# Masked key tiles and gate columns by small SBUF-to-SBUF transfers on the SP queue, with corrected planner durations

## The chip, the cores and the metric

The kernel runs on one core of one Trainium2 chip (trn2). The metric is the device time of one execution in microseconds. All runs quoted are of the fast state, as far as the state of a one-core run can be told: no run was over 1.5% above the fastest of its kernel.

Engines are called as in the profile. PE is TensorE, PEld its weight loads, DVE is VectorE, ACT is ScalarE, POOL is GpSimd. SP is SyncE; here it does nothing but issue transfers, in order, and wait for semaphores.

## The reference, cut to what matters

The input is x of 2048 tokens by 512. Two branches are mixed by a gate per token, `g = sigmoid(sum(x * gate_w))`:

```python
# branch A: attention with 32 heads of 16, in 4 chunks (L = 512), with a running memory
logits = einsum('bhqd,bhkd->bhqk', qs, ks) * scale + mask     # causal inside the chunk
a_dot  = einsum('bhqk,bhkd->bhqd', softmax(logits), vs)
num    = einsum('bhld,bhde->bhle', phi(qs), M)                # memory read; phi = elu + 1
den    = einsum('bhld,bhd->bhl', phi(qs), z)
o      = sig(beta) * num / (den + 1e-6) + (1 - sig(beta)) * a_dot
M, z   = M + phi(ks)^T vs, z + sum(phi(ks))                   # memory update
# branch B: relu-gated feed-forward, 512 -> 1792 -> 512
# out = g * A + (1 - g) * B
```

The score matmuls use TensorE in row groups of 32 (the profile's form `32*128`), and a head has only 16 rows. So each pair of heads shares a row group, and the key tile of one head of a pair has the rows of the other set to zero: these are the masked key tiles `kp`. A gate column is the gate of a token laid out as the attention output has its tokens (`gexpT`).

Of the kernel before, what the change touches and what calls it, by code (L numbers as in the profile page):

```python
# [54 lines left out]

class Op:
    __slots__ = ("engs", "eng", "fns", "occs", "lat", "reads", "writes", "name", "dma", "nbytes", "mode", "ep", "role",
                 "after", "preds", "stream", "idx", "start", "end", "done", "cidx", "gate")

    def __init__(self, alts, reads=(), writes=(), name="", lat=0.0, dma=False, nbytes=0, mode="f", ep=None, role=None):  # L60
        self.engs = [a[0] for a in alts]
        self.fns = {a[0]: a[1] for a in alts}
        self.occs = {a[0]: float(a[2]) for a in alts}
        self.eng = self.engs[0] if len(alts) == 1 else None
        self.lat = lat
        self.reads = tuple(reads)
        self.writes = tuple(writes)
        self.name = name
        self.dma = dma
        self.nbytes = nbytes  # L70
        self.mode = mode
        self.ep = ep
        self.role = role
        self.after = 0.0
        self.preds = []
        self.gate = None
        self.stream = self.idx = self.start = self.end = None
        self.done = False
        if ep is not None:
            if role == "r":  # L80
                ep.readers.append(self)
                self.reads = self.reads + (ep.res,)
            else:
                self.writes = self.writes + (ep.res,)


class Sched:
# [3 lines left out]
    def __init__(self, ndma=16, nbanks=4):  # L91
        self.bank_ep = [None] * nbanks
        self.ndma = ndma
        self.streams = list(self.ENGS) + [f"dma{i}" for i in range(ndma)]
        self.cnt = {s: 0 for s in self.streams}
        self.know = {e: {s: 0 for s in self.streams} for e in self.ENGS}
        self.snap = {s: {0: {t: 0 for t in self.streams}} for s in self.streams}
        self.res = {}
        self.now = {e: 800.0 for e in self.ENGS}
        self.mode = "f"  # L100
        self.queues = {e: [] for e in self.ENGS}
        self.dma_rr = 0
        self.dma_end = {}
        self.dma_busy = 0.0
        self.prog = {e: [] for e in self.ENGS}
        self.busy = {e: 0.0 for e in self.ENGS}
        self.ops = []
        self.log = []
        self.sem = {}
# [126 lines left out]
    def _waits(self, e, deps):  # L236
        for st, idx in sorted(deps.items(), key=lambda kv: (kv[0] == e, kv[0])):
            if idx <= 0 or self.know[e][st] >= idx:
                continue
            self.prog[e].append(("wait", st, 16 * idx if st.startswith("dma") else idx))  # L240
            kn = self.know[e]
            for k2, v2 in self.snap[st][idx].items():
                if v2 > kn[k2]:
                    kn[k2] = v2
            kn[st] = max(kn[st], idx)

    def place(self, op, e, start):
# [18 lines left out]
        if op.dma:  # L266
            d = min(range(self.ndma), key=lambda i: (self.dma_end.get(i, 0.0), i))
            st = f"dma{d}"
            if self.cnt[st] > 0:
                self._waits(e, {st: self.cnt[st]})  # L270
            self.cnt[st] += 1
            inc = 16
            issued = start + occ
            self.dma_busy = max(self.dma_busy, issued) + op.nbytes / 340.0
# [65 lines left out]
    def emit(self, block):  # L340
        sec = {"pe": block.tensor, "act": block.scalar, "dve": block.vector, "pool": block.gpsimd, "sp": block.sync}
        for e in self.ENGS:
            def body(engobj, prog=self.prog[e], e=e):
                for item in prog:
                    if item[0] == "wait":
                        engobj.wait_ge(self.sem[item[1]], item[2])
                    else:
                        _, op, st, inc = item
                        op.fns[e](engobj).then_inc(self.sem[st], inc)
            sec[e](body)  # L350


# [39 lines left out]
def program(sc, nc, T, PL, PA, A_x, A_wq, A_wk, A_wv, A_wo, A_beta, W_g, W_u, W_d, gate_w, out, NSEG, KT, NF, NT, EPS, SCALE):  # L392
# [132 lines left out]
    gw_act = act(lambda e: e.activation(V.gwc[:], A(ep_w)[:, 0:KT], ACT.Copy), 180, writes=["gwc"], name="gwc", ep=ep_w, role="r")  # L525
    gw_pe.after = 9000.0
    gexpT_r = {}
    gq = {"pe": [], "act": [], "dve": [], "flex": [], "sp": []}
    for c in range(NSEG):
        t0, t1 = 4 * c, 4 * c + 4  # L530
        gx = V.gexp[:, t0:t1]
# [20 lines left out]
        gq["dve"].append(dve(lambda e, om=om: e.reciprocal(om, om), 250, reads=[f"omg1{c}"], writes=[f"omg{c}"], name="omg"))  # L552
        gexpT_r[c] = []
        for a in range(4):
            for jj in range(4):
                dst = V.gexpT[32 * jj:32 * jj + 32, :].rearrange("q (t a) -> q t a", a=4)[:, t0:t1, a]
                gq["flex"].append(sc.add(Op([("dve", lambda e, a=a, dst=dst, t0=t0, t1=t1: e.tensor_copy(dst, V.gexp[32 * a:32 * a + 32, t0:t1]), 150),  # L557
                                             ("act", lambda e, a=a, dst=dst, t0=t0, t1=t1: e.activation(dst, V.gexp[32 * a:32 * a + 32, t0:t1], ACT.Copy), 215)],
                                            reads=[f"gexp{c}"], writes=[f"gexpT{c}_{a}{jj}"], name="gexpT")))
                gexpT_r[c].append(f"gexpT{c}_{a}{jj}")  # L560

    def c2g(s):
        t0 = 4 * s
# [2 lines left out]
    sc.queue(3, [gw_pe] + gq["pe"])  # L566
    sc.queue(1, [gw_act] + gq["act"])
    sc.queue(1, gq["dve"])
    sc.queue(2, gq["flex"])
    sc.queue(3, gq["sp"])  # L570

    def kslot(s, n):
# [5 lines left out]
    def proj(s):  # L578
# [17 lines left out]
        for G in range(4):  # L596
# [2 lines left out]
            evs.append(dve(lambda e, ep=ep, qs=qs: e.tensor_copy(V.qT[:, qs, :], A(ep)[:, :]), t_dve(512), writes=[f"qT{qs}"], name=f"qcp{s}_{G}", ep=ep, role="r"))  # L599
            if s > 0:  # L600
                acts.append(act(lambda e, qs=qs, G=G: e.activation(V.phiq[:, G, :], V.qT[:, qs, :], ACT.Exp), t_act(512, False), reads=[f"qT{qs}"], writes=[f"phiq{G}"], name=f"qexp{s}_{G}"))
                sbs.append(dve(lambda e, qs=qs, G=G: e.tensor_scalar(V.ttmp[:, G % 2, :], V.qT[:, qs, :], 0.0, 1.0, ALU.max, ALU.add), t_dve(512, 4), reads=[f"qT{qs}"], writes=[f"ttmp{G % 2}"], name=f"qts{s}_{G}"))
                sbs.append(dve(lambda e, G=G: e.tensor_tensor(V.phiq[:, G, :], V.phiq[:, G, :], V.ttmp[:, G % 2, :], ALU.min), t_dve(512, 2), reads=[f"phiq{G}", f"ttmp{G % 2}"], writes=[f"phiq{G}"], name=f"qphi{s}_{G}"))
            ep = pj(V.wk, G, "k", "wk")
            evs.append(dve(lambda e, ep=ep, G=G: e.tensor_copy(V.kT[:, G, :], A(ep)[:, :]), t_dve(512), writes=[f"kT{G}"], name=f"kcp{s}_{G}", ep=ep, role="r"))
            for p in range(2):
                ks = kslot(s, 2 * G + p)
                km = lambda e, G=G, p=p, ks=ks: e.tensor_scalar(V.kp[:, ks, :], V.kT[:, G, :], V.pm[:, p:p + 1], None, ALU.mult)  # L608
                alts = [("dve", km, 390)] + ([("pool", km, 680)] if s else [])
                evs.append(sc.add(Op(alts, reads=[f"kT{G}", "pm"], writes=[f"kp{ks}"], name=f"kmask{s}_{G}_{p}")))  # L610
            if s < NSEG - 1:
                acts.append(act(lambda e, G=G: e.activation(V.ek[:, G, :], V.kT[:, G, :], ACT.Exp), t_act(512, False), reads=[f"kT{G}"], writes=[f"ek{G}"], name=f"kexp{s}_{G}"))
                sbs.append(dve(lambda e, G=G: e.tensor_scalar(V.ttmp[:, G % 2, :], V.kT[:, G, :], 0.0, 1.0, ALU.max, ALU.add), t_dve(512, 4), reads=[f"kT{G}"], writes=[f"ttmp{G % 2}"], name=f"kts{s}_{G}"))
                sbs.append(dve(lambda e, G=G: e.tensor_tensor(V.ek[:, G, :], V.ek[:, G, :], V.ttmp[:, G % 2, :], ALU.min), t_dve(512, 2), reads=[f"ek{G}", f"ttmp{G % 2}"], writes=[f"ek{G}"], name=f"kphi{s}_{G}"))
                sps.append(dma("sp", lambda e, G=G: e.dma_start_transpose(V.phik[:, :, G * 128:(G + 1) * 128], V.ek[:, G, :]), 1 << 17, occ=1280.0, reads=[f"ek{G}"], writes=[f"phik{G}"], name=f"kT2{s}_{G}"))
        for tt in range(4):
            ep = pj(V.wv, tt, "v", "wv", True)
# [61 lines left out]
    def att(s, between):  # L679
# [23 lines left out]
        def flush():  # L703
# [22 lines left out]
            rv = V.rden[:, :].rearrange("q (p c) -> q p c", p=2)  # L726
            gv = V.rdg[:, :].rearrange("q (p c) -> q p c", p=2)
            ds.append(dve(lambda e: e.reciprocal(rv, Tv[:, :, :, 16]), 345, reads=["Tn0", "Tn1"], writes=["rden"], name=f"rden{s}_{G}"))
            ds.append(dve(lambda e: e.tensor_tensor(gv, rv, V.gexpT[:, 16 * s:16 * s + 16].unsqueeze(1).to_broadcast([128, 2, 16]), ALU.mult), 264, reads=["rden"] + gexpT_r[s], writes=["rdg"], name=f"rdg{s}_{G}"))
            av = V.adT[:, :].rearrange("q (c p e) -> q p c e", p=2, e=16)  # L730
            ds.append(dve(lambda e: e.tensor_tensor(av, Tv[:, :, :, 0:16], gv.unsqueeze(3).to_broadcast([128, 2, 16, 16]), ALU.mult), 806, reads=["Tn0", "Tn1", "rdg"], writes=["adT"], name=f"ad{s}_{G}"))
            os_ = (s % 2) * 4 + G
            if s == 0:
                ds.append(dve(lambda e: e.transpose(V.oT[:, os_, :], V.adT[:, :]), t_dve(512), reads=["adT"], writes=[f"oT{os_}"], name=f"bt{s}_{G}"))
            else:
                ds.append(dve(lambda e: e.transpose(V.oTt[:, :], V.adT[:, :]), t_dve(512), reads=["adT"], writes=["oTt"], name=f"bt{s}_{G}"))  # L736
                ds.append(dve(lambda e: e.tensor_tensor(V.oT[:, os_, :], V.oTt[:, :], V.amemT[:, G, :], ALU.add), t_dve(512, 2), reads=["oTt"] + [f"amemT{i}" for i in range(4)], writes=[f"oT{os_}"], name=f"oa{s}_{G}"))
            return pair

        for G in range(4):  # L740
# [137 lines left out]
        sc.queue(2, [t for t in Q["dsb"] if t.name.startswith(px)])  # L878
    sc.queue(0, Q["pool"])
    sc.queue(1, Q["poolmu"])  # L880
    sc.queue(1, Q["spk"])
    sc.queue(1, Q["spa"])
    sc.queue(1, Q["spo"])
    n = {id(t) for e in sc.ENGS for q in sc.queues[e] for t in q[1]}
# [1 line left out]
    sc.run()  # L886
    for i in sorted(range(sc.ndma), key=lambda i: sc.dma_end.get(i, 0.0)):
        if sc.cnt[f"dma{i}"]:
            sc.prog["sp"].append(("wait", f"dma{i}", 16 * sc.cnt[f"dma{i}"]))


def bass_gated_mix__memory_aug_infini_attn__glu_gated_reglu__prompt_kernel(
# [31 lines left out]
```

## The kernel before: what the change touches

The kernel is planned in Python when it is built. Every operation is an `Op` with the engines that may do it, a believed duration for each, and what it reads and writes. A greedy planner simulates the engines and fixes the order of instructions on each of them, and where an engine waits for a semaphore. At run time the lists stay as they are: each engine, and SP's queue, has its list and takes it in order. A believed duration therefore changes the choice of engine and the order, and nothing else.

The masks are two tensor-times-column products per group of 128 key rows, on DVE in chunk 0 and on DVE or POOL afterwards:

```python
evs.append(dve(... tensor_copy(V.kT[:, G, :], A(ep)[:, :]) ...))          # keys out of PSUM
for p in range(2):
    ks = kslot(s, 2 * G + p)                                              # 12 slots, used in turn
    km = lambda ...: e.tensor_scalar(V.kp[:, ks, :], V.kT[:, G, :], V.pm[:, p:p + 1], None, ALU.mult)
    alts = [("dve", km, 390)] + ([("pool", km, 680)] if s else [])
    evs.append(sc.add(Op(alts, reads=[f"kT{G}", "pm"], writes=[f"kp{ks}"], ...)))
# phi(k) = min(exp(k), max(k, 0) + 1): ACT, DVE, DVE; then SP transposes it for the memory update
acts.append(act(... activation(V.ek[:, G, :], V.kT[:, G, :], ACT.Exp) ...))
sbs.append(dve(... tensor_scalar(V.ttmp[:, G % 2, :], V.kT[:, G, :], 0.0, 1.0, ALU.max, ALU.add), t_dve(512, 4), ...))
sbs.append(dve(... tensor_tensor(V.ek[:, G, :], V.ek[:, G, :], V.ttmp[:, G % 2, :], ALU.min), t_dve(512, 2), ...))
sps.append(dma("sp", ... dma_start_transpose(V.phik[:, :, G * 128:(G + 1) * 128], V.ek[:, G, :]), occ=1280.0, ...))
# ... (cut)
```

The gate columns are sixteen copies of 32 partitions by 4 values per chunk, on DVE or ACT:

```python
for a in range(4):
    for jj in range(4):
        dst = V.gexpT[32 * jj:32 * jj + 32, :].rearrange("q (t a) -> q t a", a=4)[:, t0:t1, a]
        gq["flex"].append(sc.add(Op([("dve", ... tensor_copy(dst, V.gexp[32 * a:32 * a + 32, t0:t1]), 150),
                                     ("act", ... activation(dst, V.gexp[32 * a:32 * a + 32, t0:t1], ACT.Copy), 215)], ...)))
```

They are used by one DVE operation per group of heads, the gate multiply `rdg`, which stands in DVE's list between everything else that DVE does. SP also issues the weight loads, the transposed x of chunks 1 to 3 (`xT`), a second plain load of x rows for the gate (`osb<-in_A_x_dram`), the transposes `phik` and `amemT`, and the output stores.

The softmax here doesn't subtract the row's maximum and nothing guards it: scores larger than these inputs give would overflow.

## Time and profile before

| | before |
|---|---|
| time, median of 6 runs | 273.77 us (273.37 to 274.14) |
| span of the profiled run | 272.4 us, TensorE clock 1.0 |
| PE busy | 264.6 us, 97% |
| DVE, ACT, POOL busy | 206.2, 196.0, 120.9 us |
| SP's time in issuing, summed from the trace | 79.1 us |

The profile page of before gives the busy time of each engine, with its share of the span and its number of instructions:

```profile
PE 264.6 (97%) x2126; PEld 115.8 (43%) x2161; DVE 206.2 (76%) x411; ACT 196.0 (72%) x194; POOL 120.9 (44%) x168
```

PE has 7.8 us in which it is not busy, and a good part of that is the start and the end. The page's chain that ended last, followed back from the end, says the same:

```profile
PE 92%; DVE 4%; issue 2%; DMA 1%; ACT 0%
PE psA L772 36%; PE psA L811 16%; PE psA L592 10%; PE psL L691 9%; PE psA L717 7%; PE psA L590 5%; PE psA L804 4%; DVE gexpT L557 1%; PE psA L665 1%; DMA hT<-in_A_x_dram 1%; PE psA L636 1%; PE psL L500 1%; PE psA L652 1%; DVE qT L599 0%; PE psL L492 0%
```

What the change takes from the engines is in the groups of instructions of before: busy time, mean ns of one, idle time just before and what ended it.

```profile
...
L608 POOL TENSOR_SCALAR kp<-kT,pm 128x512 bf16<-128x512 bf16 x16 | 27.3, 1708 | 1.4 <-PE psL L691 0.8 <-DVE kT L605 0.4
...
L608 DVE TENSOR_SCALAR kp<-kT,pm 128x512 bf16<-128x512 bf16 x16 | 6.8, 430 | 1.3 <-PE psL L691 1.3
...
L558 ACT ACTIVATE gexpT<-gexp 32x4 f32<-32x4 f32 x40 | 8.3, 206 | 1.0
...
L557 DVE COPY gexpT<-gexp 32x4 f32<-32x4 f32 x24 | 5.8, 240 | 0.7
```

One mask takes 430 ns on DVE and 1,708 ns on POOL, where the planner believes 680.

The next view is the SP queue of before in order of time: start, length, engine, line, what is issued and how many times.

```profile
22.52 1.33 SPq L425 DMA_DIRECT2D wd<-in_B_W_down_dram  x1
23.90 5.97 SPq L444 DMA_TRANSPOSE xT<-in_A_x_dram  x2
32.23 1.22 SPq L615 DMA_TRANSPOSE phik<-ek  x1
33.49 4.21 SPq L444 DMA_TRANSPOSE xT<-in_A_x_dram  x3
40.62 1.22 SPq L615 DMA_TRANSPOSE phik<-ek  x1
41.88 1.26 SPq L444 DMA_TRANSPOSE xT<-in_A_x_dram  x1
43.18 1.26 SPq L615 DMA_TRANSPOSE phik<-ek  x1
44.49 2.56 SPq L444 DMA_TRANSPOSE xT<-in_A_x_dram  x2
47.09 1.53 SPq L544 DMA_DIRECT2D osb<-in_A_x_dram  x1
49.15 1.22 SPq L615 DMA_TRANSPOSE phik<-ek  x1
55.53 0.35 SPq L544 DMA_DIRECT2D osb<-in_A_x_dram  x1
60.80 1.66 SPq L615 DMA_TRANSPOSE phik<-ek  x1
```

(A line joins like issues that follow each other, pauses between them included.) A transpose occupies SP for 1.2 us. A plain transfer takes 0.33 to 0.35 us when SP had been waiting, and mostly about 0.58 us straight after a transpose. Each phik transpose starts as soon as its input is there: comparing the end of the twelve `ek` min operations with the start of the twelve phik issues in the trace, the delay is 0.11 us on average and 0.5 us at most. SP is idle most of the time after 50 us.

### The profile page before, as it was taken

To read this page: it belongs to the slowest core of one execution; us is meant where nothing else is said; L and a number is where in the kernel's file an instruction comes from. 1 tells how busy PE (TensorE), PEld (TensorE's weight loads), DVE (VectorE), ACT (ScalarE), POOL (GpSimd) and SP (SyncE) were. 2 spreads that over 40 slices of the span, in tenths; PEclk is the share of its full clock that TensorE was granted. 3 is DMA by queue.
4 is the path that set the end of the run, shared out by engine and by line. 5 is a ranking of instruction groups with operands and counts; after the bars stand their busy time and mean duration, and the time that the engine had idled before them with its cause. 6 is when DMAs were issued, how large, how long until landed. Compare 5 with 4: busy or idle time off the path is not lost.

```text
span 272.4 us, 5341 instructions
## 1 busy us (share of the span) xinstructions
PE 264.6 (97%) x2126; PEld 115.8 (43%) x2161; DVE 206.2 (76%) x411; ACT 196.0 (72%) x194; POOL 120.9 (44%) x168
## 2 busy tenths in 40 slices
PE   8999999999998999999999999999999999999996
PEld 5444434443443443443435343434344343444445
DVE  4789999999999989998987958885956274957200
ACT  3279898898798778888878977977887676952122
POOL 5023397879495374934364743243433333320000
PEclk9999999999999999999999999999999999999999
DMA  7999934301200234100113110100120000000011
GB/s 231 272 361 207 282 60 92 45 23 39 59 2 1 61 77 99 39 22 0 23 21 76 41 58 22 40 1 0 22 45 17 28 30 23 0 2 0 0 41 39
DMA packets 31025, 17.01 MB, mean 62 GB/s; under 512 B 20760, under 2 KB 31000, under 8 KB 31000
## 3 DMA queue, kind: packets, MB, share of 16 engines
q1 hardware_dynamic: 30416, 16.14, 23.9%
q10 hardware_dynamic: 584, 0.53, 0.7%
q8 instruction: 17, 0.28, 0.4%
q14 instruction: 8, 0.07, 0.1%
HBM read 9.84 MB, written 2.10 MB: 44 GB/s over the span
## 4 chain that ended last, share of the span: by engine, by line
PE 92%; DVE 4%; issue 2%; DMA 1%; ACT 0%
PE psA L772 36%; PE psA L811 16%; PE psA L592 10%; PE psL L691 9%; PE psA L717 7%; PE psA L590 5%; PE psA L804 4%; DVE gexpT L557 1%; PE psA L665 1%; DMA hT<-in_A_x_dram 1%; PE psA L636 1%; PE psL L500 1%; PE psA L652 1%; DVE qT L599 0%; PE psL L492 0%
## 5 line engine op out<-in xcount | busy, mean ns | idle before, releaser
L696 ACT ACTIVATE E<-psL 128x2048 bf16<-128x2048 f32 x80 | 150.0, 1875 | 33.6 <-PE psL L691 32.4
L699 POOL TENSOR_SCALAR_AFFINE_SELECT E<-E 128x512 bf16<-128x512 bf16 x128 | 83.4, 671 | 116.6 <-ACT E L696 111.9
L772 PE MATMUL psA<-xT,wu 128*128 128x512 bf16 x216 | 58.5, 380 | 0.7 <-issue 0.3
L772 PE MATMUL psA<-xT,wg 128*128 128x512 bf16 x213 | 57.2, 380 | 1.1 <-issue 0.8
L811 PE MATMUL psA<-wd,hT 128*128 128x512 bf16 (+1 forms) x230 | 53.0, 367 | 0.8 <-issue 0.6
L783 DVE TENSOR_TENSOR hT<-psA,rl 128x512 bf16<-128x512 f32 x56 | 38.0, 680 | 10.5 <-PE psA L772 10.2
L811 PEld LDWEIGHTS psA<-wd,hT 128*128 128x128 bf16 x238 | 21.6, 98 | 24.0 <-issue 3.8
L691 PE MATMUL psL<-qT,kp 32*128 32x384 bf16 (+3 forms) x512 | 31.7, 301 | 0.0
L780 ACT ACTIVATE rl<-psA 128x512 bf16<-128x512 f32 x34 | 20.3, 597 | 15.2 <-PE psA L772 11.2
L772 PEld LDWEIGHTS psA<-xT,wg 128*128 128x128 bf16 x224 | 20.2, 98 | 25.0 <-issue 3.1
L772 PEld LDWEIGHTS psA<-xT,wu 128*128 128x128 bf16 x224 | 20.3, 98 | 24.8 <-issue 2.0
L608 POOL TENSOR_SCALAR kp<-kT,pm 128x512 bf16<-128x512 bf16 x16 | 27.3, 1708 | 1.4 <-PE psL L691 0.8
L722 DVE STREAM_TRANSPOSE Tn<-psA 128x512 f32<-128x512 f32 x32 | 21.0, 692 | 6.7 <-PE psA L717 6.7
L691 PEld LDWEIGHTS psL<-qT,kp 32*128 32x128 bf16 x512 | 8.9, 92 | 33.5 <-ACT E L696 15.7
L717 PE MATMUL psA<-E,vaug 128*17 128x256 bf16 (+3 forms) x512 | 20.2, 300 | 0.0
L820 DVE TENSOR_SCALAR osb<-psA,omg 128x512 bf16<-128x512 f32 x10 | 7.4, 744 | 14.1 <-PE psA L811 14.1
L781 DVE TENSOR_SCALAR rl<-psA 128x512 bf16<-128x512 f32 x22 | 15.1, 687 | 3.8 <-PE psA L772 3.5
L592 PE MATMUL psA<-xT,wq 128*128 128x512 bf16 x62 | 16.3, 384 | 0.2 <-issue 0.2
L804 PE MATMUL psA<-wo,oT 128*128 128x512 bf16 (+1 forms) x67 | 16.2, 366 | 0.2 <-DVE oTt L736 0.2
L592 PE MATMUL psA<-xT,wk 128*128 128x512 bf16 x60 | 15.8, 380 | 0.3 <-issue 0.2
L590 PE MATMUL psA<-wv,xT 128*128 128x512 bf16 x63 | 15.5, 380 | 0.1
L717 PEld LDWEIGHTS psA<-E,vaug 128*17 128x17 bf16 x512 | 10.7, 90 | 9.6 <-issue 2.7
(74 smaller groups left out, 236.9 us busy)
## 6 DMA issues: line engine op xcount, KB each, us to landing
out_dram<-osb SPq DMA_DIRECT2D x15, 128.0 KB, 1.7
wg<-in_B_W_gate_dram SPq DMA_DIRECT2D x8, 224.0 KB, 6.1
wu<-in_B_W_up_dram SPq DMA_DIRECT2D x8, 224.0 KB, 6.5
wd<-in_B_W_down_dram SPq DMA_DIRECT2D x1, 1792.0 KB
osb<-in_A_x_dram SPq DMA_DIRECT2D x12, 128.0 KB, 2.2
wk<-in_A_wk_dram SPq DMA_DIRECT2D x4, 128.0 KB, 4.0
wv<-in_A_wv_dram SPq DMA_DIRECT2D x4, 128.0 KB, 3.6
wo<-in_A_wo_dram SPq DMA_DIRECT2D x1, 512.0 KB, 5.4
```

Of the source, the lines that this page charges most:

```text
L590: ins = e.matmul(A(ep)[:, :], lhsT=V.xT[:, kt, tok + col * 128:tok + (col + 1) * 128], rhs=w[:, kt, :], start=(kt == 0), stop=(kt == KT - 1))
L592: ins = e.matmul(A(ep)[:, :], lhsT=w[:, kt, col * 128:(col + 1) * 128], rhs=V.xT[:, kt, tok:tok + 512], start=(kt == 0), stop=(kt == KT - 1))
L608: km = lambda e, G=G, p=p, ks=ks: e.tensor_scalar(V.kp[:, ks, :], V.kT[:, G, :], V.pm[:, p:p + 1], None, ALU.mult)
L691: ins = q.matmul(PL[:, jj, o:o + w], lhsT=V.kp[32 * jj:32 * jj + 32, kslot(s, n), 128 * j:128 * j + 128], rhs=V.qT[32 * jj:32 * jj + 32, q ...
L696: acts.append(act(lambda a, e=e: a.activation(V.E[:, e, :, :], PL[:, :, :], ACT.Exp, scale=SCALE), t_act(2048), reads=[f"bankL{b}" for b i ...
L699: pools.append(pool(lambda g, ap=ap: g.affine_select(out=ap, in_=ap, compare_op=ALU.is_ge, fill=0.0, base=0, pattern=[[0, 4], [1, 128]], c ...
L717: ins = q.matmul(A(ep)[32 * jj:32 * jj + 17, c:512], lhsT=V.vaug[:, s % 2, j, 8 * G + 2 * jj + p, :], rhs=V.E[:, e, jj, o:o + w], start=(j ...
L722: ds.append(dve(lambda e, p=p, ep=eps[p]: e.transpose(V.Tn[:, p, :], A(ep)[:, :]), t_dve(512), writes=[f"Tn{p}"], name=f"tr{s}_{G}_{p}", e ...
L772: ins = e.matmul(A(ep)[:, :], lhsT=w[:, kt, f * 128:(f + 1) * 128], rhs=V.xT[:, kt, c * 512:(c + 1) * 512], start=(kt == 0), stop=(kt == K ...
L783: evs.append(dve(lambda e, ep=eu, r=r, hs=hs: e.tensor_tensor(V.hT[:, hs, :], A(ep)[:, :], V.rl[:, r, :], ALU.mult), t_dve(512), reads=[f" ...
L804: ins = e.matmul(A(ep)[:, 0:c1 - c0], lhsT=V.oT[:, o0 + G, i * 128:(i + 1) * 128], rhs=V.wo[:, G, c0:c1], start=st_ and G == 0, stop=sp_ a ...
L811: ins = e.matmul(A(ep)[:, 0:c1 - c0], lhsT=V.hT[:, slots[f], i * 128:(i + 1) * 128], rhs=V.wd[:, f, c0:c1], start=st_ and f == f0, stop=sp ...
```

## The change

The intent is to free DVE, ACT and POOL. For chunks 1 (its second half) to 3 a masked key tile is made by four transfers on SP, each copying 16 rows of every 32 into a slot whose other rows are already zero; the first twelve masks, on DVE, leave those zeros. Gate columns are four transfers for each of four quarters of a chunk. The Trainium skill, "DMA: Bandwidth & Descriptors", Rules for kernel authors, says why it takes four each: an access pattern on SBUF whose inner dimension steps whole partitions is mis-addressed, so blocks of partitions need separate transfers. The planner counts a group of four as one operation of 4 x 450 ns on SP (`nd = 4`), and places masks ahead of phik on SP. Some believed durations of DVE operations are corrected towards what traces show. Plumbing is cut:

```diff
-            for jj in range(4):
-                dst = V.gexpT[32 * jj:32 * jj + 32, :].rearrange("q (t a) -> q t a", a=4)[:, t0:t1, a]
-                gq["flex"].append(sc.add(Op([("dve", ... 150), ("act", ... 215)], ...)))
+            gd = lambda e, ...: [e.dma_start(V.gexpT[r:r + 32, 16 * c + 4 * a:16 * c + 4 * a + 4], V.gexp[32 * a:32 * a + 32, t0:t1]) for r in range(0, 128, 32)]
+            t = dma("sp", gd, 1 << 13, occ=4 * 450.0, reads=[f"gexp{c}"], writes=[f"gexpT{c}_{a}"], ...)
+            t.nd = 4
+            gq["sp"].append(t)
@@
-                alts = [("dve", km, 390)] + ([("pool", km, 680)] if s else [])
-                evs.append(sc.add(Op(alts, ...)))
+                if s * 8 + 2 * G + p < 12:
+                    evs.append(dve(km, 420, ...))
+                else:
+                    kd = lambda e, ...: [e.dma_start(V.kp[r:r + 16, ks, :], V.kT[r:r + 16, G, :]) for r in range(16 * p, 128, 32)]
+                    t = dma("sp", kd, 1 << 16, occ=4 * 450.0, reads=[f"kT{G}"], writes=[f"kp{ks}"], ...)
+                    t.nd = 4
+                    sps.append(t)
@@  durations: max-add of q and k t_dve(512, 4) -> 330; min of q and k, and the add of oT,
@@  t_dve(512, 2) -> 540; adT 806 -> 870; rdg 264 -> 310 (new layout of gexpT); mask 390 -> 420
@@
-    sc.queue(1, Q["spk"])
+    sc.queue(0, [t for t in Q["spk"] if t.nd > 1])
+    sc.queue(1, [t for t in Q["spk"] if t.nd == 1])
```

More of the change, by code (lines that the diff above doesn't have):

```diff
@@ L57 @@
     __slots__ = ("engs", "eng", "fns", "occs", "lat", "reads", "writes", "name", "dma", "nbytes", "mode", "ep", "role",
-                 "after", "preds", "stream", "idx", "start", "end", "done", "cidx", "gate")
+                 "after", "preds", "stream", "idx", "start", "end", "done", "cidx", "gate", "nd")
     def __init__(self, alts, reads=(), writes=(), name="", lat=0.0, dma=False, nbytes=0, mode="f", ep=None, role=None):
@@ L76, in __init__ @@
         self.gate = None
+        self.nd = 1
         self.stream = self.idx = self.start = self.end = None
@@ L103, in __init__ @@
         self.dma_end = {}
+        self.semval = {}
         self.dma_busy = 0.0
@@ L239, in _waits @@
                 continue
-            self.prog[e].append(("wait", st, 16 * idx if st.startswith("dma") else idx))
+            self.prog[e].append(("wait", st, self.semval[st, idx] if st.startswith("dma") else idx))
             kn = self.know[e]
@@ L271, in place @@
             self.cnt[st] += 1
+            self.semval[st, self.cnt[st]] = self.semval.get((st, self.cnt[st] - 1), 0) + 16 * op.nd
             inc = 16
@@ L348, in body @@
                         _, op, st, inc = item
-                        op.fns[e](engobj).then_inc(self.sem[st], inc)
+                        res = op.fns[e](engobj)
+                        for r in (res if op.nd > 1 else [res]):
+                            r.then_inc(self.sem[st], inc)
             sec[e](body)
@@ L527, in program @@
     gexpT_r = {}
-    gq = {"pe": [], "act": [], "dve": [], "flex": [], "sp": []}
+    gq = {"pe": [], "act": [], "dve": [], "sp": []}
     for c in range(NSEG):
@@ L554, in program @@
         for a in range(4):
-            for jj in range(4):
-                dst = V.gexpT[32 * jj:32 * jj + 32, :].rearrange("q (t a) -> q t a", a=4)[:, t0:t1, a]
-                gq["flex"].append(sc.add(Op([("dve", lambda e, a=a, dst=dst, t0=t0, t1=t1: e.tensor_copy(dst, V.gexp[32 * a:32 * a + 32, t0:t1]), 150),
-                                             ("act", lambda e, a=a, dst=dst, t0=t0, t1=t1: e.activation(dst, V.gexp[32 * a:32 * a + 32, t0:t1], ACT.Copy), 215)],
-                                            reads=[f"gexp{c}"], writes=[f"gexpT{c}_{a}{jj}"], name="gexpT")))
-                gexpT_r[c].append(f"gexpT{c}_{a}{jj}")
+            gd = lambda e, a=a, c=c, t0=t0, t1=t1: [e.dma_start(V.gexpT[r:r + 32, 16 * c + 4 * a:16 * c + 4 * a + 4], V.gexp[32 * a:32 * a + 32, t0:t1]) for r in range(0, 128, 32)]
+            t = dma("sp", gd, 1 << 13, occ=4 * 450.0, reads=[f"gexp{c}"], writes=[f"gexpT{c}_{a}"], name=f"gexpT{c}")
+            t.nd = 4
+            gq["sp"].append(t)
+            gexpT_r[c].append(f"gexpT{c}_{a}")
     def c2g(s):
@@ L568, in program @@
     sc.queue(1, gq["dve"])
-    sc.queue(2, gq["flex"])
     sc.queue(3, gq["sp"])
@@ L601, in proj @@
                 acts.append(act(lambda e, qs=qs, G=G: e.activation(V.phiq[:, G, :], V.qT[:, qs, :], ACT.Exp), t_act(512, False), reads=[f"qT{qs}"], writes=[f"phiq{G}"], name=f"qexp{s}_{G}"))
-                sbs.append(dve(lambda e, qs=qs, G=G: e.tensor_scalar(V.ttmp[:, G % 2, :], V.qT[:, qs, :], 0.0, 1.0, ALU.max, ALU.add), t_dve(512, 4), reads=[f"qT{qs}"], writes=[f"ttmp{G % 2}"], name=f"qts{s}_{G}"))
-                sbs.append(dve(lambda e, G=G: e.tensor_tensor(V.phiq[:, G, :], V.phiq[:, G, :], V.ttmp[:, G % 2, :], ALU.min), t_dve(512, 2), reads=[f"phiq{G}", f"ttmp{G % 2}"], writes=[f"phiq{G}"], name=f"qphi{s}_{G}"))
+                sbs.append(dve(lambda e, qs=qs, G=G: e.tensor_scalar(V.ttmp[:, G % 2, :], V.qT[:, qs, :], 0.0, 1.0, ALU.max, ALU.add), 330, reads=[f"qT{qs}"], writes=[f"ttmp{G % 2}"], name=f"qts{s}_{G}"))
+                sbs.append(dve(lambda e, G=G: e.tensor_tensor(V.phiq[:, G, :], V.phiq[:, G, :], V.ttmp[:, G % 2, :], ALU.min), 540, reads=[f"phiq{G}", f"ttmp{G % 2}"], writes=[f"phiq{G}"], name=f"qphi{s}_{G}"))
             ep = pj(V.wk, G, "k", "wk")
@@ L607, in proj @@
                 ks = kslot(s, 2 * G + p)
-                km = lambda e, G=G, p=p, ks=ks: e.tensor_scalar(V.kp[:, ks, :], V.kT[:, G, :], V.pm[:, p:p + 1], None, ALU.mult)
-                alts = [("dve", km, 390)] + ([("pool", km, 680)] if s else [])
-                evs.append(sc.add(Op(alts, reads=[f"kT{G}", "pm"], writes=[f"kp{ks}"], name=f"kmask{s}_{G}_{p}")))
+                if s * 8 + 2 * G + p < 12:
+                    km = lambda e, G=G, p=p, ks=ks: e.tensor_scalar(V.kp[:, ks, :], V.kT[:, G, :], V.pm[:, p:p + 1], None, ALU.mult)
+                    evs.append(dve(km, 420, reads=[f"kT{G}", "pm"], writes=[f"kp{ks}"], name=f"kmask{s}_{G}_{p}"))
+                else:
+                    kd = lambda e, G=G, p=p, ks=ks: [e.dma_start(V.kp[r:r + 16, ks, :], V.kT[r:r + 16, G, :]) for r in range(16 * p, 128, 32)]
+                    t = dma("sp", kd, 1 << 16, occ=4 * 450.0, reads=[f"kT{G}"], writes=[f"kp{ks}"], name=f"kpd{s}_{G}_{p}")
+                    t.nd = 4
+                    sps.append(t)
             if s < NSEG - 1:
                 acts.append(act(lambda e, G=G: e.activation(V.ek[:, G, :], V.kT[:, G, :], ACT.Exp), t_act(512, False), reads=[f"kT{G}"], writes=[f"ek{G}"], name=f"kexp{s}_{G}"))
-                sbs.append(dve(lambda e, G=G: e.tensor_scalar(V.ttmp[:, G % 2, :], V.kT[:, G, :], 0.0, 1.0, ALU.max, ALU.add), t_dve(512, 4), reads=[f"kT{G}"], writes=[f"ttmp{G % 2}"], name=f"kts{s}_{G}"))
-                sbs.append(dve(lambda e, G=G: e.tensor_tensor(V.ek[:, G, :], V.ek[:, G, :], V.ttmp[:, G % 2, :], ALU.min), t_dve(512, 2), reads=[f"ek{G}", f"ttmp{G % 2}"], writes=[f"ek{G}"], name=f"kphi{s}_{G}"))
+                sbs.append(dve(lambda e, G=G: e.tensor_scalar(V.ttmp[:, G % 2, :], V.kT[:, G, :], 0.0, 1.0, ALU.max, ALU.add), 330, reads=[f"kT{G}"], writes=[f"ttmp{G % 2}"], name=f"kts{s}_{G}"))
+                sbs.append(dve(lambda e, G=G: e.tensor_tensor(V.ek[:, G, :], V.ek[:, G, :], V.ttmp[:, G % 2, :], ALU.min), 540, reads=[f"ek{G}", f"ttmp{G % 2}"], writes=[f"ek{G}"], name=f"kphi{s}_{G}"))
                 sps.append(dma("sp", lambda e, G=G: e.dma_start_transpose(V.phik[:, :, G * 128:(G + 1) * 128], V.ek[:, G, :]), 1 << 17, occ=1280.0, reads=[f"ek{G}"], writes=[f"phik{G}"], name=f"kT2{s}_{G}"))
@@ L728, in flush @@
             ds.append(dve(lambda e: e.reciprocal(rv, Tv[:, :, :, 16]), 345, reads=["Tn0", "Tn1"], writes=["rden"], name=f"rden{s}_{G}"))
-            ds.append(dve(lambda e: e.tensor_tensor(gv, rv, V.gexpT[:, 16 * s:16 * s + 16].unsqueeze(1).to_broadcast([128, 2, 16]), ALU.mult), 264, reads=["rden"] + gexpT_r[s], writes=["rdg"], name=f"rdg{s}_{G}"))
+            ge = V.gexpT[:, 16 * s:16 * s + 16].rearrange("q (a t) -> q t a", t=4).unsqueeze(1).to_broadcast([128, 2, 4, 4])
+            ds.append(dve(lambda e: e.tensor_tensor(gv.rearrange("q p (t a) -> q p t a", a=4), rv.rearrange("q p (t a) -> q p t a", a=4), ge, ALU.mult), 310, reads=["rden"] + gexpT_r[s], writes=["rdg"], name=f"rdg{s}_{G}"))
             av = V.adT[:, :].rearrange("q (c p e) -> q p c e", p=2, e=16)
-            ds.append(dve(lambda e: e.tensor_tensor(av, Tv[:, :, :, 0:16], gv.unsqueeze(3).to_broadcast([128, 2, 16, 16]), ALU.mult), 806, reads=["Tn0", "Tn1", "rdg"], writes=["adT"], name=f"ad{s}_{G}"))
+            ds.append(dve(lambda e: e.tensor_tensor(av, Tv[:, :, :, 0:16], gv.unsqueeze(3).to_broadcast([128, 2, 16, 16]), ALU.mult), 870, reads=["Tn0", "Tn1", "rdg"], writes=["adT"], name=f"ad{s}_{G}"))
             os_ = (s % 2) * 4 + G
@@ L736, in flush @@
                 ds.append(dve(lambda e: e.transpose(V.oTt[:, :], V.adT[:, :]), t_dve(512), reads=["adT"], writes=["oTt"], name=f"bt{s}_{G}"))
-                ds.append(dve(lambda e: e.tensor_tensor(V.oT[:, os_, :], V.oTt[:, :], V.amemT[:, G, :], ALU.add), t_dve(512, 2), reads=["oTt"] + [f"amemT{i}" for i in range(4)], writes=[f"oT{os_}"], name=f"oa{s}_{G}"))
+                ds.append(dve(lambda e: e.tensor_tensor(V.oT[:, os_, :], V.oTt[:, :], V.amemT[:, G, :], ALU.add), 540, reads=["oTt"] + [f"amemT{i}" for i in range(4)], writes=[f"oT{os_}"], name=f"oa{s}_{G}"))
             return pair
@@ L888, in program @@
         if sc.cnt[f"dma{i}"]:
-            sc.prog["sp"].append(("wait", f"dma{i}", 16 * sc.cnt[f"dma{i}"]))
+            sc.prog["sp"].append(("wait", f"dma{i}", sc.semval[f"dma{i}", sc.cnt[f"dma{i}"]]))
 def bass_gated_mix__memory_aug_infini_attn__glu_gated_reglu__prompt_kernel(
```

## The prediction

> **What bounds it now.** TensorE. On the profile page PE is busy 264.6 of 272.4 us (97%) at full clock; the chain of waits is 92% PE, 4% DVE. In the trace's start times, full-width matmuls follow each other every 216 ns; I compared every spacing with that. The excess: 3.7 us before the first transposes (first x load), some 3 us of warm-up, about 16 us for entering and leaving the 80 row-tiled score bursts (95 and 105 ns each; the Trainium skill, "TensorEngine Tiling (Array Packing)", Key Properties, says that changing the tiling mode drains TensorE; these gaps agree), some 3 us for the 16 value pairs, and about 3 us after the last matmul. True stalls are under 1.5 us: one of 0.74 us at 86.5 us (denominator matmuls waiting on phiq). The other waits in the wait view are nearly all weight loads held 0.4 us or less under running matmuls, or engines with slack.
>
> **What the change does.**
> - POOL loses 16 key masks: 27.3 us, 1,708 ns each (planner: 680). DVE loses 4 masks (430 ns) and 24 gate copies (5.8 us), ACT 40 gate copies (8.3 us). Two relus move to DVE, three output scalings to ACT. Net about -8 us DVE, -7 ACT, -27 POOL. The masks and DVE's bf16 work also lengthen each other (min 540 to 576 ns, max-add 340). The Trainium skill, "SBUF — State Buffer", on the exclusive GpSimd/Vector port pair, states such blocking; the 1,708 ns agrees.
> - SP gains 144 small transfers at 0.33 to 0.58 us of issue (stores and x loads in the trace): 48 to 80 us of a mostly idle queue. Landing about 2 us after issue (stores 1.7, x loads 2.2).
> - TensorE does the same matmuls in another order; score-to-value adjacencies go from 14 to 13 (+0.1 us).
>
> **On the critical path.** Almost nothing removed is on it. The floor is the PE stream, so the gain is at most the stalls, 0.7 to 1.5 us. The risk lies at 30 to 40 us: chunk 0's sixteen gate transfers stand on SP right behind the 1.8 MB wd load, four of them after the first phik transpose. Before, the issue after wd took 4.0 us and landed at 33.2 us; that phik transpose was issued at 32.2. I expect the last gate column at 36 to 39 us, where the first gate multiply (36.4 us before) wants it. DVE, in order, may stand 0 to 2 us and cost PE up to 1 us through late PSUM evacuation. Key transfers of chunks 1 to 3 have several us of slack.
>
> **Prediction.** 273.7 us, 8 in 10 between 272.4 and 276.5. Faster by over 2%: 0.01; within 2%: 0.94; slower: 0.05.
>
> **What shows each step.** PE busy 263 to 266 us (97%); DVE near 197, ACT 189, POOL 92; DVE max-add and min groups 10 to 25% shorter; POOL idles as much longer as its work falls. The wait view shows DVE's gate multiply waiting 0 to 2 us for a DMA once, in chunk 0, and no score burst waiting for a key transfer. The burst gaps remain.
>
> **What would make it wrong.** Under 271.5: PE's spacing depended on other engines' load. Over 277: SP's in-order queue, with transfers issuing at over 0.6 us or landing after 4 us, held back phik or amemT transposes or key tiles at a chunk's start (PE idle for microseconds at 70 to 180 us), or gate columns stopped DVE in every chunk.

## The result

| | before | after |
|---|---|---|
| time, median of 6 runs | 273.77 us | 291.29 us (289.48 to 292.67) |
| span of the profiled run | 272.4 us | 290.7 us |
| mean granted TensorE clock | 1.0 | 0.982 |
| SP's time in issuing | 79.1 us | 166.0 us |

The change made the kernel slower: the ratio is 1.0637, 95% interval 1.0591 to 1.0683. Here and below a ratio is that of one kernel's fast runs to the other's in the same rounds, so it is not quite the ratio of the medians. Each experiment's table entry is its median beside its own ratio.

Busy time on the page of after:

```profile
PE 269.7 (93%) x2124; PEld 117.2 (40%) x2161; DVE 195.4 (67%) x382; ACT 189.4 (65%) x155; POOL 93.4 (32%) x152
```

DVE, ACT and POOL lost about what was predicted. PE was idle for 290.7 - 269.7 = 21.0 us in place of 7.8, which is 13.2 us more, and busy for 5.1 us more. (Both traces miss nearly the same number of matmul records, so the two can be compared.) The sum, 18.3 us, is the whole difference of the spans. The chain of after has what was not there before:

```profile
PE 81%; DMA 7%; DVE 6%; SPq 3%; issue 2%; ACT 0%; DVEq 0%
PE psA L781 29%; PE psA L820 17%; PE psA L595 8%; PE psL L699 8%; PE psA L725 6%; PE psA L813 5%; PE psA L593 4%; DMA phik<-ek 3%; SPq L560 2%; DMA gexpT<-gexp 2%; DMA osb<-in_A_x_dram 2%; PE psA L644 1%; PE psL L497 1%; PE psA L673 1%; DVE kT L608 1%
```

SP's issuing and the landing of phik, gate columns and x rows are now on it. The wait view of after names who waited for them (us in total, times, longest us):

```profile
...
DVE rdg L738 <- DMA gexpT<-gexp: 7.7, 2, 4.4
...
DVE osb L552 <- DMA osb<-in_A_x_dram: 7.1, 4, 3.7
ACT ek L620 <- DMA phik<-ek: 6.9, 4, 2.5
...
PE psA L644 <- DMA phik<-ek: 4.8, 3, 1.9
...
PE psA L813 <- DVE hT L792: 3.1, 1, 3.1
...
PE psA L595 <- DVE Tn L730: 2.6, 1, 2.6
```

In the wait view of before no engine waits for any transfer but two of the first loads:

```profile
ACT eb L514 <- DMA braw<-in_A_beta_dram: 4.4, 1, 4.4
...
PEld psL L500 <- DMA hT<-in_A_x_dram: 1.1, 1, 1.1
...
PE psL L500 <- DMA hT<-in_A_x_dram: 0.2, 1, 0.2
```

The last two lines of after are consequences: DVE stood at a load of x rows before 165.35 us, and at a gate column before 120.08 us, and PE then waited for the DVE work behind it. PE does not wait for a key tile anywhere. The SP queue of after over the stretch shown for before:

```profile
22.70 11.15 SPq L560 DMA_DIRECT2D gexpT<-gexp  x12
33.97 1.24 SPq L623 DMA_TRANSPOSE phik<-ek  x1
35.25 2.48 SPq L560 DMA_DIRECT2D gexpT<-gexp  x4
37.77 5.18 SPq L449 DMA_TRANSPOSE xT<-in_A_x_dram  x4
43.00 1.26 SPq L623 DMA_TRANSPOSE phik<-ek  x1
44.31 5.01 SPq L615 DMA_DIRECT2D kp<-kT  x8
49.36 2.04 SPq L623 DMA_TRANSPOSE phik<-ek  x1
51.45 2.57 SPq L449 DMA_TRANSPOSE xT<-in_A_x_dram  x2
54.12 5.42 SPq L615 DMA_DIRECT2D kp<-kT  x8
59.59 1.26 SPq L623 DMA_TRANSPOSE phik<-ek  x1
```

Every piece begins where the one before it ends, and inside the pieces the trace has one pause over 0.15 us, of 0.45 us: SP issues almost without a break. The delay of the twelve phik issues after their inputs is 5.9 us on average and 11.5 us at most, in place of 0.11 and 0.5. That is more than the slack: the first three memory updates start 0.05 to 0.14 us after their later phik tile has landed, and before them PE waits 1.1, 1.8 and 1.9 us, the 4.8 us of the wait view. A small transfer costs SP 589 ns (masks) and 668 ns (gate columns; the first of these, right behind the wd load, took 3.7 us) on average, and 0.51 to 0.53 us even when SP had been waiting. The landing itself is quick: the page gives 1.8 and 1.7 us.

Most of the 5.1 us of longer busy time is a lowered clock. The windows view of after around the two lowered stretches (columns: length, PE busy and count, granted clock, DMA share, GB/s):

```profile
...
74.47:77.89 3.42, 1.00 (x6) 1.00 0.26 55
118.84:122.26 3.42, 2.22 (x27) 1.00 0.40 82
122.26:125.67 3.41, 1.83 (x9) 1.00 0.29 93
...
163.22:166.63 3.41, 1.38 (x7) 1.00 0.21 53
166.63:170.05 3.42, 2.38 (x13) 0.53 0.40 83
```

The clock record has half speed from 78.1 us for 3.4 us and from 166.8 us for 6.8 us, so the windows shown end 0.2 us before the drops. PE was busy for 9.4 of these 10.2 us; full-width matmuls start 427 ns apart there and 216 ns apart at full clock, so the clock accounts for about half of the 9.4, or 4.7 of the 5.1 us. The drops came after the windows in which PE was busy for 1.00 and 1.38 us (1.10 and 1.19 in windows that end exactly at the drops), and not after those with 2.22 and 1.83. The Trainium skill, "TensorE: Matmul & The Clock Gate", Part 1, tells of the half clock and of windows of 3.4 us; the lengths agree.

### The profile page after: what moved, and what is told of

It is laid out like the page before. It is cut to its first block, busy times and chain, and to the rows that moved or that the text cites. A ratio compares the mean times of both kernels' runs of the same rounds, so it can differ in the third digit from the quotient of the medians.

```text
span 290.7 us, 5430 instructions
## 1 busy us (share of the span) xinstructions
PE 269.7 (93%) x2124; PEld 117.2 (40%) x2161; DVE 195.4 (67%) x382; ACT 189.4 (65%) x155; POOL 93.4 (32%) x152
## 4 chain that ended last, share of the span: by engine, by line
PE 81%; DMA 7%; DVE 6%; SPq 3%; issue 2%; ACT 0%; DVEq 0%
PE psA L781 29%; PE psA L820 17%; PE psA L595 8%; PE psL L699 8%; PE psA L725 6%; PE psA L813 5%; PE psA L593 4%; DMA phik<-ek 3%; SPq L560 2%; DMA gexpT<-gexp 2%; DMA osb<-in_A_x_dram 2%; PE psA L644 1%; PE psL L497 1%; PE psA L673 1%; DVE kT L608 1%
## 5 line engine op out<-in xcount | busy, mean ns | idle before, releaser
L781 PE MATMUL psA<-xT,wg 128*128 128x512 bf16 x213 | 59.8, 383 | 1.2 <-issue 0.6
L820 PE MATMUL psA<-wd,hT 128*128 128x512 bf16 (+1 forms) x227 | 54.6, 375 | 1.2 <-issue 1.0
L781 PEld LDWEIGHTS psA<-xT,wu 128*128 128x128 bf16 x224 | 21.0, 99 | 27.5 <-issue 3.0
L781 PEld LDWEIGHTS psA<-xT,wg 128*128 128x128 bf16 x224 | 19.5, 98 | 24.8 <-issue 5.2
L789 ACT ACTIVATE rl<-psA 128x512 bf16<-128x512 f32 x32 | 19.1, 596 | 14.9 <-PE psA L781 14.3
L790 DVE TENSOR_SCALAR rl<-psA 128x512 bf16<-128x512 f32 x24 | 16.5, 687 | 5.5 <-PE psA L781 5.1
L813 PE MATMUL psA<-wo,oT 128*128 128x512 bf16 (+1 forms) x66 | 16.9, 381 | 3.2 <-DVE hT L792 3.1
L830 ACT ACTIVATE osb<-psA,omg 128x512 bf16<-128x512 f32 (+1 forms) x10 | 6.4, 643 | 13.6 <-PE psA L813 13.3
L593 PE MATMUL psA<-wv,xT 128*128 128x512 bf16 x61 | 14.8, 380 | 0.5 <-issue 0.5
L552 DVE CUSTOM_DVE_ANT_0 osb<-osb,gwb 128x512 bf16<-128x512 bf16 x12 | 9.6, 804 | 7.1 <-DMA osb<-in_A_x_dram 7.1
## 6 DMA issues: line engine op xcount, KB each, us to landing
out_dram<-osb SPq DMA_DIRECT2D x15, 128.0 KB, 1.7
osb<-in_A_x_dram SPq DMA_DIRECT2D x12, 128.0 KB, 2.2
wk<-in_A_wk_dram SPq DMA_DIRECT2D x4, 128.0 KB, 4.1
```

Source lines behind the costliest of these rows:

```text
L593: ins = e.matmul(A(ep)[:, :], lhsT=V.xT[:, kt, tok + col * 128:tok + (col + 1) * 128], rhs=w[:, kt, :], start=(kt == 0), stop=(kt == KT - 1))
L781: ins = e.matmul(A(ep)[:, :], lhsT=w[:, kt, f * 128:(f + 1) * 128], rhs=V.xT[:, kt, c * 512:(c + 1) * 512], start=(kt == 0), stop=(kt == K ...
L789: evs.append(sc.add(Op([("act", lambda e, ep=eg, r=r: e.activation(V.rl[:, r, :], A(ep)[:, :], ACT.Relu), t_act(512)), ("dve", lambda e, e ...
L813: ins = e.matmul(A(ep)[:, 0:c1 - c0], lhsT=V.oT[:, o0 + G, i * 128:(i + 1) * 128], rhs=V.wo[:, G, c0:c1], start=st_ and G == 0, stop=sp_ a ...
L820: ins = e.matmul(A(ep)[:, 0:c1 - c0], lhsT=V.hT[:, slots[f], i * 128:(i + 1) * 128], rhs=V.wd[:, f, c0:c1], start=st_ and f == f0, stop=sp ...
```

## The experiments

Theory A: SP is an in-order queue that this change fills. A small transfer occupies it for about 0.6 us, and what stands behind, phik above all, comes late. The rivals: the corrected durations made a worse order (B); only one of the two kinds of transfer is at fault (C, D); it is the wait for the transfers' landing (E); it is bytes and the wait for masks and not the count (F); it is only the order on SP (G).

One rival runs through all experiments: every kernel is planned anew, so that engines and SP get another order with each edit. Only one pair of runs, e3 and e12, keeps the order of every engine; it is read under e12.

All results, up to 144 transfers by SP's summed issuing time in the profiled run, then by time, and e6 last:

| run | small transfers on SP | SP issuing, us | time, us | ratio to before, 95% interval |
|---|---|---|---|---|
| before | 0 | 79.1 | 273.77 | |
| e1 durations | 0 | 77.4 | 273.75 | 0.9986 (0.997 to 1.0003) |
| e10 POOL's duration too | 0 | 78.9 | 274.00 | 1.0003 (0.9989 to 1.0018) |
| e8 paired masks, no gates | 40 | 102.6 | 275.43 | 1.0051 (1.0036 to 1.0066) |
| e2 gates only | 64 | 114.9 | 274.51 | 1.0018 (1.0002 to 1.0034) |
| e3 masks only | 80 | 128.0 | 277.30 | 1.012 (1.0091 to 1.0148) |
| e7 paired masks, gates | 104 | 140.8 | 278.69 | 1.0154 (1.0106 to 1.0202) |
| e12 masks, unread for gates | 144 | 166.2 | 279.09 | 1.0182 (1.0125 to 1.0238) |
| e5 all unread | 144 | 167.6 | 282.45 | 1.0295 (1.0248 to 1.0342) |
| e11 gates, unread for masks | 144 | 166.2 | 284.01 | 1.0357 (1.033 to 1.0383) |
| e4 true issue time in the plan | 144 | 167.3 | 286.04 | 1.0439 (1.0405 to 1.0473) |
| e9 the same, phik first | 144 | 166.1 | 287.44 | 1.0505 (1.0481 to 1.0529) |
| after | 144 | 166.0 | 291.29 | 1.0637 (1.0591 to 1.0683) |
| e6 masks issued by POOL | 64 (80 on POOL) | 116.8 | 289.89 | 1.0557 (1.0522 to 1.0592) |

### e1_durations: the durations alone

```diff
 # the kernel before, planner durations of after; no transfers
-alts = [("dve", km, 390)] + ([("pool", km, 680)] if s else [])
+alts = [("dve", km, 420)] + ([("pool", km, 680)] if s else [])
 # and 330, 540, 540, 870 for max-add, min, add and adT
```

> The kernel before with the corrected planner durations alone; masks and gate columns stay on their engines. Theory A (SP's in-order queue is overloaded by 144 small transfers of about 0.6 us of issue each, and phik transposes, gate columns and x loads come late): 272.5 to 275.5 us, no phik or gate wait in the wait view, clock 1.0. Rival B (the new durations make a worse order): over 280 us, with PE stalls like those of after.

Measured: 273.75 us, clock 1.0, no wait for phik or a gate column. The order of the instructions changed and the time did not, so B falls: the slowdown comes with the transfers.

### e2_gates and e3_masks: each kind alone

```diff
 # e2: after, but
+alts = [("dve", km, 420)] + ([("pool", km, 680)] if s else [])     # all masks on engines again
 # e3: after, but
+gq["flex"].append(...)                                             # gate columns copied on DVE and ACT again
```

> The changed kernel with the masks back on DVE and POOL; only the 64 gate transfers (about 40 us of SP) are new, and the durations. Theory A: between before and after, about 277 to 284 us, with the DVE gate multiply waiting for a gate column in chunk 0 (about 3 us) and PE idle after it; phik waits mostly gone. Rival B: as slow as after, 288 to 293 us. Rival C (only the mask transfers are to blame): 273 to 275 us.

> The changed kernel with the gate columns copied on DVE and ACT again; only the 80 mask transfers (about 50 us of SP) are new, and the durations. Theory A: about 277 to 284 us, with phik waits at the memory-update matmuls still there and no gate wait. Rival B: 288 to 293 us. Rival D (only the gate transfers are to blame): 273 to 275 us.

Measured: 274.51 and 277.30 us. The gates alone cost far less than I expected (0.7 us, expected some 3 to 10), though the signs are there in its wait view:

```profile
DVE rdg L733 <- DMA gexpT<-gexp: 2.5, 1, 2.5
...
PE psA L639 <- DMA phik<-ek: 1.8, 1, 1.8
```

Phik came over 7 us late three times in chunk 0 of e2, and PE waited for it 1.8 us in all: the slack took the rest. The masks alone cost 3 us, as expected. DVE waits 5.7 us for the x rows behind the masks on SP. I had expected phik as a releaser, and the profile names it nowhere; but its memory-update matmuls at 125.5 us start after 1.8 us without a releaser ("issue"), and in the trace the phik transpose that stood on SP from 121.4 to 124.2 us, behind eight mask transfers, lands at 125.41 us, 0.09 us before them. So this was a phik wait too. Neither C nor D holds, since the two costs together are some 4 us and after shows 17. That the loss grows faster than the load because SP can no longer catch up is not shown: the six kernels with 166 to 168 us of issuing lose 5 to 17 us.

### e4_true_issue and e9_phik_first: would a better plan carry the load?

```diff
-occ=4 * 450.0
+occ=4 * 630.0          # e4 and e9, both kinds of transfer
 # e9 in addition:
-sc.queue(0, masks); sc.queue(1, phik); sc.queue(1, amemT)
+sc.queue(2, masks); sc.queue(0, phik); sc.queue(0, amemT)
```

> The changed kernel, its transfers and their number as they are; the planner alone is told the measured issue time, 630 ns instead of 450 ns for each small transfer. Theory A in the form A1 (the plan's wrong issue time is what hurts, SP could carry the load): 273 to 279 us, waits for phik and gate columns under 4 us in total. Form A2 (the load itself is too much at the chunk boundaries whatever the plan): 282 to 292 us. Rival B: no change, 288 to 293 us.

> The run with the true issue time (286.0 us) and, in addition, the SP priorities turned round: phik and amemT transposes before mask transfers. All 144 transfers remain. Theory A2 (the load itself is too much): whichever goes first, the others come late: phik waits shrink to under 1 us, but score bursts and gate multiplies wait instead, and the time stays at 280 us or more. Rival G (only the order on SP, with masks ahead of phik, is at fault): 273 to 277 us.

Measured: 286.04 and 287.44 us. The planner's wrong issue time is worth about 5 of the 17 us; the rest stays (form A2). With phik first, PE hardly waits for phik any more (0.3 us, in e4 2.5), but DVE waits 7.9 us for gate columns (in e4 3.5). The score bursts wait for E to be released by ACT in both (PE idle 6.1 us, in e4 6.5; in after 0.9). The time is no better. Rival G falls: whatever goes first, something else is late.

### e5_useless, e11 and e12: SP's load without the dependence

e5 has the work of before with e1's durations (and the gate-column layout of after). In addition SP issues the 144 transfers with 8 bytes a row, from a constant tile to a scratch tile that nobody reads. They have the triggers, priorities and believed times of the real ones.

```diff
+def useless(after):
+    t = dma("sp", lambda e, n=n: [e.dma_start(V.dum[32 * i:32 * i + 16, 4 * n:4 * n + 4], V.ident[32 * i:32 * i + 16, 0:4]) for i in range(4)], ..., occ=4 * 450.0, ...)
+    t.nd = 4
+    t.preds.append((after, False))     # waits for the key copy or the gate, as the real one; nothing waits for it
+    return t
 # e11: gate transfers real, masks on DVE and POOL with 80 unread transfers
 # e12: mask transfers real, gate columns on DVE and ACT with 64 unread transfers
```

> The work of the kernel before with the corrected durations: masks and gate columns stay on DVE, ACT and POOL. In addition SP issues 144 transfers of 8 bytes a row that nobody reads, planned like the changed kernel's (same triggers, same priorities, same believed 450 ns). Theory A (SP's issue time by itself does the harm, by holding back what stands behind it in the queue): over 277 us, up to 290, with SP issuing nearly without a pause at 20 to 80 us and waits for phik, amemT or x loads back. Rival E (the harm comes from waiting for the transfers themselves, their landing some 2 us later than a copy on an engine): 273 to 275.5 us, as without them.

> The 64 gate transfers are real, the 80 mask transfers are the unread ones and the masks are made on DVE and POOL: SP has the changed kernel's load, but no score burst depends on it. With nothing awaited the load cost 8.7 us (282.45 against 273.75), with everything awaited 17.5. Theory A with the two shares adding: between them, 282 to 288 us, with the gate multiply waiting for its columns again. If it is 290 us or more, the gate columns are the whole second share; if it is 282 us or less, it is the mask tiles.

> The counterpart of the run with real gate and unread mask transfers: the 80 mask transfers are real, the gate columns are copied on DVE and ACT, and 64 unread transfers take the place of the gate transfers on SP. If the shares of the slowdown add (load alone 6.9 us at full clock, real gates 3, real masks 3, and up to 5 us of lowered TensorE clock on top where stalls cluster): 281 to 289 us in all, 281 to 285 with the part of the lowered clock taken off, no gate wait in the wait view. At 277 us or less the shares do not add and the real gate columns are the main thing.

Measured: e5 282.45 us, that is 8.7 us over e1, for transfers that nobody reads. Its wait view:

```profile
DVE osb L561 <- DMA osb<-in_A_x_dram: 13.9, 5, 6.4
...
ACT ek L630 <- DMA phik<-ek: 3.8, 2, 2.6
PE psA L654 <- DMA phik<-ek: 3.3, 2, 2.1
```

The phik delay is 4.4 us on average here, against 0.21 us in e1. This is the central result: filling SP's queue, with nothing waiting for the new transfers, is enough to make PE wait. Rival E is not needed for half of the loss. It also shows on whom the queue acts: the loads and transposes that were there before. But the planner counted these transfers too and gave e5 another order than e1, so the 8.7 us are load and new order together.

e11 gives 284.01 us and the gate wait is back (5.8 us in two waits). e12 gives 279.09 us, less than e5, where I expected 281 or more. The traces of e3 and e12 show the same order of instructions on every engine, and on SP but for the 64 unread transfers. So this pair alone shows the load by itself: 277.30 to 279.09 us, about 1.8 us for 64 transfers, with phik delayed by 3.1 us on average in place of 1.4. (The rounds differ, and the intervals of the two ratios overlap a little; no run of e12 was as fast as any of e3.) The shares do not add up, and I can't divide the remaining 9 us between gate columns and mask tiles. With the same load of 166 to 168 us the six kernels spread over 279 to 291 us, and each has a different order: the size of the loss is set by load and order together. Part of the spread is the clock: in the profiled runs it was 1.0 in e12, 0.994 in e5, 0.988 in e4 and e9, and 0.982 in after (e11 is listed with 1.0, but its trace holds no clock record; its other runs have 0.988 to 1.0).

### e7_paired and e8_paired_masks: half the count, the same bytes

```diff
-kd = ... [e.dma_start(V.kp[r:r + 16, ks, :], V.kT[r:r + 16, G, :]) for r in range(16 * p, 128, 32)]
+kd = ... [e.dma_start(V.kp[r:r + 16, k0:k0 + 3:2, :], V.kT[r:r + 16, G - 1:G + 1, :]) for r in range(16 * p, 128, 32)]   # odd G only, occ 4 * 620
 # e8: in addition gate columns on DVE and ACT again
```

> The changed kernel with each two mask transfers of neighbouring groups joined in one of twice the size: 40 of them instead of 80, same bytes; 64 gate transfers as they are; planned at 620 ns each for the masks. Theory A: the count on SP is what matters, so between the run with masks alone (277.3) and well under after: 276 to 283 us. Rival F (bytes or the wait for mask tiles matter): 286 us and more, as the mask tiles now land later.

> As the run before, with the gate columns copied on DVE and ACT again: 40 transfers in all on SP. Theory A: 273 to 275 us, no DMA wait of a us or more on PE, DVE or ACT after the first 20 us. Rival F: 277 us and more, like the run with 80 mask transfers.

Measured: 278.69 and 275.43 us. Two mask tiles in one transfer cost SP 631 ns on average, where one tile cost 589 ns (the medians are 593 and 589, and 589 in e5 with 8 bytes a row): the count is what costs SP its time, not the bytes, and F falls. Joining 80 transfers into 40 took off 12.6 us of the 17.5, although half of the tiles now wait for the group after them. (e7 also has the truer issue time in its plan for the masks, so a part of this may be the plan's.) e8 landed 0.4 us above the range that I gave it, with no long DMA wait, as expected; even 40 transfers are no gain over none.

### e6_pool_issue: another queue

```diff
-t = dma("sp", kd, 1 << 16, occ=4 * 450.0, ...)
+t = dma("pool", kd, 1 << 16, occ=4 * 1000.0, ...)      # with its own semaphores
```

> The changed kernel with the 80 mask transfers issued by POOL, planned at 1 us each; the 64 gate transfers stay on SP. Theory A: SP's load falls to that of the run with gate transfers alone, and the time with it, 274 to 278 us, unless POOL in turn gets late with its own masks (then POOL is seen as the releaser of value matmuls). Rival E: the landing is no sooner, so 285 us and more.

Measured: 289.89 us, a miss for theory A as I put it. POOL issued the four transfers of a mask in 1.94 us without trouble, and SP issued for only 116.8 us. But the planner, with POOL's list changed, put two phik transposes behind four stores, four x loads and eight gate transfers on SP, and SP mostly stood waiting at the head of its list: these two were issued 37 us after their inputs were ready. So SP's order did the harm without SP being busy. The run shows that a low sum of issuing is not sufficient; it doesn't tell what POOL's queue would give under a good plan. That stays open. The planner saw it coming: its own simulated end was 283.2 us, against 269.3 for before (more on this below).

### e10_pool_time: is there anything to gain?

```diff
-("pool", km, 680)
+("pool", km, 1700)     # e1 with POOL's mask as measured
```

> The kernel before with all durations corrected, POOL's mask too (1,700 ns instead of 680), no transfers. Nothing that a better plan can save is larger than the TensorE stalls of before (0.7 to 1.5 us): 272.8 to 274.3 us, that is 0.995 to 1.001 of before; a gain of 2 us or more would refute the reading that TensorE is at its floor.

Measured: 274.00 us, the same as before. No kernel here beats before. The experiments don't point to one either: PE's own list is the limit, and none of the parts of the change shortens that list.

## Why the prediction was wrong

- **"TensorE bounds it; almost nothing removed is on the critical path": right.** Taking about 11 us from DVE, 7 from ACT and 27 from POOL gained nothing, and e1 and e10 gained nothing by better plans. DVE, ACT and POOL came out at 195.4, 189.4 and 93.4 us, predicted near 197, 189 and 92.
- **"48 to 80 us of a mostly idle queue": the step that failed.** The term was 89.9 us (80 x 589 ns + 64 x 668 ns). The trace of before already had 0.58 us for a plain issue straight after a transpose, and the 144 transfers come in groups of four and more; I used the whole range down to 0.33 us, the rate of stores and x loads after a wait, where small transfers took 0.51 to 0.53 us even then. Worse, I spread the sum over the whole span. SP had issued for 8 to 10 us of every 10 up to 30 us and for 5 to 9 up to 50 us before the change, and afterwards it issued for 8 to 9.6 us of every 10 up to 80 us. Much of the free time was after 200 us, where almost nothing was added.
- **"Key transfers of chunks 1 to 3 have several us of slack": right and beside the point.** No score burst waited for a key transfer. What came too late was behind them in the same list: phik, whose slack of 3.3 to 5.9 us was less than delays of up to 11.5 us, the x rows and the gate columns. PE waited 4.8 us for phik, and more for DVE, which stood at x rows and gate columns. I asked when each new transfer had to land and not what each one would hold back. I named SP's in-order queue holding back phik as what could make the prediction wrong, with issue over 0.6 us as its sign, and gave it too small a chance.
- **"DVE may stand 0 to 2 us, once, in chunk 0": too small.** It stood 3.3 us there and 4.4 us in another chunk. In chunk 0 the last four gate transfers were issued up to 37.7 us and landed at 38.9 us. That landing lies in my range of 36 to 39 us; DVE had come to wait for it earlier, at 35.8 us.
- **"PE busy 263 to 266 us": wrong by the clock.** It came out at 269.7 us. I did not consider that the clock drops after windows with long stalls. That added about 4.7 us in the profiled run.
- **"Max-add and min 10 to 25% shorter": mostly right.** The min operations went from 576 and 539 ns to 498 and 471, the max-add of q from 336 to 298, but the max-add of k from 347 to 455. The blocking that the prediction cites shows in the trace of before: min operations with no POOL operation beside them took 407 to 426 ns, with one up to 868. POOL's 1,708 ns is another matter: its shortest mask took 1,560 ns. The burst gaps of about 95 ns in and 100 out stayed, as predicted.

Why the planner's own list was so bad is shown only in part: the true issue time in the plan (e4) took off about 5 us. Building the kernels again and reading the planner's own simulated end adds to this (planner figures, not chip times): 269.3 us for before and 269.4 for after, so the plan saw none of the 17 us; 280.9 for e4 and 280.1 for e9, so with 630 ns this planner itself finds no order that hides the load. How much a better search could remove is open.

## What to carry to other kernels

Before moving work to a transfer queue, add up the issuing time in the stretch where the new transfers fall, at the back-to-back rate and by count, not by bytes. Then ask of every transfer behind them in that queue how much slack it has, from its landing to its use: the queue here passed its delay on to everything behind. In this kernel, with TensorE 97% busy, relief for other engines gained nothing, while its stalls were paid a second time when the clock dropped.

## What the Trainium skill lacked or had wrong

- "DMA: Bandwidth & Descriptors" (Anatomy of one DMA — SWDGE (gpsimd) path) says of transfers issued by POOL that the fixed cost is completion latency and not setup, with a dispatch of about 50 ns, and (Issuing engines are not separate DMA queues) that the time to initiate a transfer is usually small relative to the transfer. It has no measured time for which an issue holds SP. The runs show on SP 0.33 to 0.35 us for a store or x load after a wait, about 0.52 us for a small SBUF-to-SBUF transfer after a wait and 0.59 us in a row, 1.2 us for a transpose, with 1.7 to 1.8 us to landing for the small ones; on POOL 0.49 us (e6). 0.59 us of 1.8 is not small, and it is the part that adds up. It hardly grows with bytes: the median is 589 ns for 16 rows of 8 bytes and of 1 KB, 593 ns for 16 rows of 2 KB.
- No page puts a number on what a queue full of small transfers holds back. 144 of them, unread, cost 8.7 us together with the new order that they caused (e5), 64 about 1.8 us with the order unchanged (e12 against e3).
- "TensorE: Matmul & The Clock Gate", Part 1, has the clock drop after an idle window, and does not say how much work a window may hold and still count as idle. Cutting the traces into windows of 3.41 us on the boundaries of their clock records, seven drops in six traces (after, e4, e5, e6, e7, e9) followed windows in which PE was busy for 0.40 to 1.37 us; the least busy windows at full clock that no drop followed had 1.50 (e4), 1.53 (e6) and 1.58 us (e2).
- "TensorEngine Tiling (Array Packing)", Key Properties, says that a change of tiling mode drains TensorE but not what that costs: in the traces of before and after about 95 ns going into a row-tiled burst of score matmuls and about 100 ns going out (317 ns from a burst's last start, 512 wide, to the next full-width one, where two full-width ones are 216 ns apart).
